# Column attention and two feed-forward layers in float32: four more outputs of the first token pair by seven products

## The chip, the core and the metric

One core of a Trainium2 chip. The metric is the device time of one execution in microseconds (us). TensorE (PE, with its weight loads PEld) does the matrix products into PSUM; VectorE (DVE) and ScalarE (ACT) read PSUM and SBUF; GpSimd (POOL) and SyncE (SP) issue DMAs here. Each engine runs its own queue in program order and waits for others by semaphores.

## The reference, cut to what matters

```python
qn = q / (norm(q, axis=1) + 1e-6);  kn = k / (norm(k, axis=1) + 1e-6)   # q, k, v: 6016 x 256
a = softmax(kn.T @ qn / tau)                                            # 256 x 256
x = v @ a
h = x @ w_in                                                            # 256 -> 2048
x = (h * sigmoid(1.702 * h)) @ w_out                                    # 2048 -> 256
h = x @ moe2_w_in
out = (max(h, 0) + alpha * min(h, 0)) @ moe2_w_out
```

All is float32.

## The kernel before

**Words.** A float32 operand is split into a high part (a rounded copy, by ScalarE) and a low part (the difference, by VectorE), and a product is three matmuls: high by high, high of the weights by low of the data, low of the weights by high of the data. The weights arrive as raw 64-bit words in 16 pieces of 128x512 for each layer (8 of W1I, the input weights, which are multiplied by the softmax first; 8 of W1O, the output weights, in `WO`), and the `Converter` turns each into such a pair: `scale` on ScalarE, then `shift`, `power`, `rest` on VectorE, then either `less` and `low` on VectorE around a ScalarE `copy` (five VectorE steps), or, for an `added` piece, an accumulating DMA on POOL's queue, and later a ScalarE `copy` and a VectorE `split` (four VectorE steps). W1I's pieces 4 to 7 and W1O's 4 to 7 are added.

**Tokens** are worked in six pairs of two column blocks (five pairs of 2x512, one of 2x448), through layer 1 and then layer 2; within a pair, over eight output groups j = 0 to 7. An output group has four outputs (two rows of 128 by two column blocks). Each output is activated by ScalarE, split (`ghi` by ScalarE L876, `glo` by VectorE L882), and multiplied by `WO` into `ps_o`; these second products (`outs.next()`, L814) of group j are emitted between the first products (L785) of group j + 1.

**Two ways of a group.** `direct` takes eight products, 24 matmuls. `quartet` is a Strassen form with seven products, 21 matmuls. It needs four sums of weights (`combine_wi`: VectorE `whole`, `sums_`, ScalarE `high`, VectorE `low`) and four differences of data, T1 to T4 (`prepare`: VectorE difference, ScalarE high, VectorE low). Its products come in the order A11·B11, S1·T1, A12·B21, S2·T2, S3·T3, A22·T4, S4·B22. In the first pair groups 0 to `STRASSEN` - 1 are direct, since weights and differences are not there yet; `STRASSEN` is 6. In the other pairs all groups are quartets.

**How W1I comes.** `emit_w(j)` (in output 1 of groups 0 to 2) and `emit_pair(j)` (outputs 13 and 21, counted 4j + i) multiply the softmax by a piece into the PSUM tile `pw`; ScalarE copies the high part from there, and VectorE makes the low part right behind (L575 and L579; L726 and L727).

**The planner.** Side work is placed at build time. After each direct output `beside(FIRST)` first emits up to `most` of the ScalarE jobs in `put_off`, then VectorE steps until a budget of 2.1 us is used; a quartet has three such places, with budgets `FREE`. Steps come from `bg` (of each kind, 0 = data, 1 = weight sums, only the oldest can go) or from the converter; the converter goes first when its `due` is not later than the step's. A load must be 3 places old before its `scale` (`LOADING`), and an accumulating DMA 3 places before its `copy` (`LANDING`). A step whose ScalarE job is still in `put_off` has to wait. `finish(steps)` emits at once what is left of the steps, wherever it stands. In the code: `LAST = 4 * STRASSEN`, and T1 to T4 are due three or four places before `LAST` and finished before the first quartet.

Of the kernel before, what the change touches and what calls it, by code (L numbers as in the profile page):

```python
# [15 lines left out]
P = 128  # L16
N = 6016
C = 256
# [12 lines left out]
FREE = ((0.7, 2.8, 1.7), (0.0, 0.8, 0.8))  # L31
FIRST = 2.1
AHEAD = 2
QK_PARTS = [1, 3] + [4] * 9 + [2, 2, 2, 1]
TAIL = 12
LOADING = 3
LANDING = 3
STRASSEN = 6
ON_VECTOR = (4, 5, 6, 8)
# [20 lines left out]
def attention_then_two_ffns(ctx: ExitStack, tc: tile.TileContext, q, k, vT, tau, w1i, w1o, w2i, w2o, alpha, outT):  # L60
# [129 lines left out]
    class Converter:  # L190


        STEPS = (("shift", 0.45), ("power", 0.45), ("rest", 0.63), ("less", 0.63), ("low", 0.63))
        ADDED = (("shift", 0.45), ("power", 0.45), ("rest", 0.63))

# [30 lines left out]
        def time(self, piece):  # L226
            if not piece or self.landed():
                return 0.63
            return self.list(piece)[self.at][1]
# [35 lines left out]
        def step(self):  # L265

            if self.waits():
                if not self.open:
                    self.scale(True)
                scalar_work()  # L270
            if not self.next() or self.landed():
                self.settle()
                return 0.63
            if not self.open:
                self.open = self.ready.pop(0)
                self.held = 1
            steps = self.list(self.open)
            do, t = steps[self.at][0], self.time(self.open)
            getattr(self.open, do)()
            self.at += 1  # L280
            if do == "rest":
                self.held = 0
                self.scale()
                if self.ahead:
                    self.load()
            if self.at == len(steps):
                if self.open.added:
                    self.open.sent()
                    self.flying.append(self.open)
                self.open, self.at = None, 0  # L290
            return t
# [17 lines left out]
        def due(self):  # L309
            return min(x.due for x in self.left())  # L310

# [19 lines left out]
    with tc.manual_schedule():  # L331
# [26 lines left out]
        def outer(j, n=1):  # L358
            def pair():
                return tuple(WO[:, j:j + n, h].rearrange("p q a b -> p q (a b)") if n > 1 else flat(WO[:, j, h]) for h in range(2))  # L360
            return Convert(w1o[:, j * PIECE:(j + n) * PIECE].rearrange("p (a n) -> p a n", a=1), pair, added=j > 3)

# [6 lines left out]
        LAST = 4 * STRASSEN  # L369
        PAIRS = {4: 13, 6: min(21, LAST - 2)}  # L370
        for j, x in ia.items():
# [237 lines left out]

        operands, xin2, combining = {}, [], []  # L610

        class Step:
# [7 lines left out]
            def waits(self):  # L620
                return self.needs in put_off

            def run(self):
                if self.waits():
                    scalar_work()
                self.do()
                if self.then:
                    put_off.append(self.then)

        def prepare(l, p):  # L630
# [20 lines left out]
            def minus(nm, a, b):  # L651
# [4 lines left out]
                ("B11", B11), ("B21", B21), ("T1", None), ("T2", None), ("T3", None), ("T4", None), ("B22", B22))}  # L656
            D = 0.63
            early = [
# [18 lines left out]
            if (l, p) == (0, 0):  # L677
                def last():
                    ops["T4"] = operand()
                    tmp["T4"] = tmp["T2"]  # L680
                    minus("T4", B21, "T2")
                steps = [early[i] for i in (2, 3, 6, 7)] + [late[0], Step(D, None, last, hi["T4"])] + [late[i] for i in (4, 5)]
                for x, due in zip(steps, (4, 4, 4, 4, 3, 3, 3, 3)):
                    x.due = LAST - due
                return steps
            return early, late

        def combine(hi, lo, hi_s, lo_s):

            box = {}  # L690

            def whole():
                t = box["t"] = cv.tile([P, 4, P], F32, tag="c", name="t", bufs=2)
                nc.vector.tensor_tensor(t, f32(hi), f32(lo), ALU.add)

            def sums_():
                t = box["t"]
                s = box["s"] = cv.tile([P, 4, P], F32, tag="c", name="s", bufs=2)
                nc.vector.tensor_tensor(s[:, 0], t[:, A21], t[:, A22], ALU.add)
                nc.vector.tensor_tensor(s[:, 1], s[:, 0], t[:, A11], ALU.subtract)  # L700
                nc.vector.tensor_tensor(s[:, 2], t[:, A11], t[:, A21], ALU.subtract)
                nc.vector.tensor_tensor(s[:, 3], t[:, A12], s[:, 1], ALU.subtract)

            def low():
                nc.vector.tensor_tensor(lo_s(), box["s"], f32(hi_s()), ALU.subtract)

            def high():
                nc.scalar.copy(hi_s(), box["s"])

            steps = [Step(0.63, None, whole, kind=1), Step(0.9, None, sums_, high, 1), Step(0.63, high, low, kind=1)]  # L710
            combining.append(steps)
            return steps

        def combine_wi(j):
            return combine(*(WI[:, j, h, :4] for h in range(2)), *(lambda h=h: WI[:, j, h, S1:] for h in range(2)))

        def emit_pair(j):

            conv.need([ia[j], ia[j + 1]])
            for m in range(2):  # L720
# [5 lines left out]
                nc.scalar.activation(hi, src, AF.Copy, scale=rs[:, m:m + 1])  # L726
                nc.vector.scalar_tensor_tensor(lo, src, rs[:, m:m + 1], f32(hi), ALU.mult, ALU.subtract)  # L727

        def emit_w(j):
# [6 lines left out]
            for m in range(2):  # L736
                if j > 1 or m:
                    keep_hi(j, m, pw, m * C)
                    keep_lo(j, m, pw, m * C)

        bg = []
        spare = [0.0]

# [6 lines left out]
        def beside(time, convert=False, place=None, most=None):  # L750

            conv.place()
            now = scalar_work(most)
            late = now if place == 0 else []
# [18 lines left out]
        def finish(steps):  # L773

            while any(s in bg for s in steps):
                s = next(x for x in bg if x in steps) if Convert.deep else bg[0]
                bg.remove(s)
                if s.waits():
                    put_off.remove(s.needs)
                    s.needs()  # L780
# [103 lines left out]
        def direct(j, outs, mid_way):  # L884
# [3 lines left out]
            for i, (f, c) in enumerate((f, c) for f in range(2) for c in range(2)):  # L888
# [11 lines left out]
                mid_way(i)  # L900
                beside(FIRST, most=2 if (j, i) == (STRASSEN - 1, 3) else 3)
                u.low()
                units.append((f, c, u.pair))
            return Outs(0, 0, j, units)

        def quartet(l, p, j, outs, carry):
# [20 lines left out]
            ends = (l, p, j) == (1, NP - 1, NQ - 1)  # L927
            most = 1 if l else 2 if narrow else None
            u11, u22, u21, u12 = (Unit(l, 2 * j + f, c) for f, c in ((0, c0), (1, c1), (1, c0), (0, c1)))
            fork = (l, p, j) != (1, 0, 0)  # L930
            a, b = bank(), bank()
            product(a, j, A11, ops["B11"], n, True, True)
# [20 lines left out]
            if j != 1:  # L953
                beside(FREE[l][0], place=0, most=most)
            if fork:
# [11 lines left out]
            if before:  # L967
                b12.low()
            outs.next()
            product(a, j, S2, ops["T2"], n, False, True)  # L970
            u2 = copy(a)
# [5 lines left out]
            outs.next()  # L977
            beside(FREE[l][1], most=most)
            finish(late[:4])
            product(a, j, S3, ops["T3"], n, False, True)  # L980
            u3 = copy(a)
# [3 lines left out]
            evacuate()  # L985
            beside(FREE[l][2], most=most)
            finish(late)
            u22.act()
            product(a, j, A22, ops["T4"], n, False, True)
# [14 lines left out]
            return Outs(l, p, j, [(0, c0, u11.pair), (1, c1, u22.pair), (1, c0, u21.pair), (0, c1, u12.pair)])  # L1004

        operands[0, 0] = blocks
        conv.ahead = True
# [27 lines left out]
        small = [flat(G), Convert.pool.tile([P, T], F32, tag="top", name="second", bufs=3)]  # L1035
        sums0, pair1 = [], []
        outs, carry = None, []
# [21 lines left out]
        def combining_of(n):  # L1059
            combined[n] = combine_wi(n)  # L1060
            for x in combined[n]:
                x.due = LAST + 3 * ((n or NQ) - STRASSEN) - 1
            bg.extend(combined[n])

        def mid_way(i):
            at = 4 * j + i
            if j < 3 and i == 1:
                if j == 0:
                    conv.need([ob_[0]])
                emit_w(j + 1)  # L1070
            for n, due in PAIRS.items():
                if at == due:
                    emit_pair(n)
                    for m in (n, n + 1):
                        if m >= STRASSEN:
                            combining_of(m)
            if j == 2 and i == 0:
                nc.sync.dma_start(alpha_sb, alpha)
            if at == LAST - 10:
                sums0.extend(prepare(0, 0))  # L1080
                bg.extend(sums0)
            if at == LAST - 2:
                combining_of(0)
            next_pair()

        for j in range(NQ):
            if j:
                conv.need([ob_[j - 1]])
            if j < STRASSEN:
                outs = direct(j, outs, mid_way)  # L1090
                continue
            finish(combined[j])
            finish(sums0)
            next_pair()
# [152 lines left out]
```

## Time and profile before

| | us |
|---|---|
| median of 3 runs (1032.49 to 1033.44) | 1032.55 |
| the profiled execution | 1033.06 |
| its span, first to last instruction | 1031.3 |
| busy PE / DVE / ACT / POOL in the span | 1025.7 / 750.5 / 758.5 / 38.4 |

A share of busy time is an average over stages; the timelines below show who waits at a place. Matmuls overlap, so their single durations (385 ns) are longer than their spacing.

### The profile page before, as it was taken

What the parts mean: (1) busy time and instruction counts of PE and PEld (TensorE: products, weight loads), DVE (VectorE), ACT (ScalarE), POOL (GpSimd) and SP (SyncE); (2) the same over time, 40 slices, a digit from 0 to 9 for tenths busy, and PEclk for the clock granted to TensorE, in tenths of its full rate; (3) what the DMA queues carried; (4) which work ended last, traced back from release to release, by engine and by line L of the source; (5) the groups of instructions that cost most, each with busy time, mean ns of one, the idle gap of its engine ahead of it and who ended that gap; (6) DMA issues with size and microseconds to landing.
All of it is one profiled execution on the core that took longest, in us unless ns stands there. A gap on an engine that the chain in (4) does not pass through costs nothing.

```text
span 1031.3 us, 12536 instructions
## 1 busy us (share of the span) xinstructions
PE 1025.7 (99%) x4634; PEld 865.4 (84%) x4634; DVE 750.5 (73%) x1226; ACT 758.5 (74%) x1273; POOL 38.4 (4%) x50
## 2 busy tenths in 40 slices
PE   9999999999999999999999999999999999999998
PEld 8888888888888888888998888888888888888997
DVE  4788888877778765445637877787877787877766
ACT  6787787778778766666767777777777777867776
POOL 4401000000000000000100000000000000000000
PEclk9999999999999999999999999999999999999999
DMA  9737222224325312003553001001001000000100
GB/s 356 266 106 178 65 74 70 98 80 168 114 89 179 113 41 77 1 1 132 196 168 113 1 21 62 1 21 62 1 21 62 1 18 25 36 0 1 41 1 36
DMA packets 32445, 79.72 MB, mean 77 GB/s; under 512 B 3200, under 2 KB 7808, under 8 KB 32384
## 3 DMA queue, kind: packets, MB, share of 16 engines
q1 hardware_dynamic: 28928, 65.29, 18.3%
q0 software_dynamic: 3456, 13.63, 4.6%
q8 instruction: 36, 0.59, 0.2%
q14 instruction: 25, 0.20, 0.1%
HBM read 52.96 MB, written 23.86 MB: 74 GB/s over the span
## 4 chain that ended last, share of the span: by engine, by line
PE 99%; DMA 0%; SPq 0%; ACT 0%; issue 0%
PE ps_o L814 50%; PE ps_h L785 44%; PE gram L433 4%; PE pw L567 1%; PE pw L723 1%; DMA qk<-in_k 0%; SPq L453 0%; PE nrm L510 0%; ACT s L831 0%; PE bc L532 0%; PE pt L555 0%
## 5 line engine op out<-in xcount | busy, mean ns | idle before, releaser
L814 PE MATMUL ps_o<-ghi,wo 128*128 128x512 f32 (+1 forms) x1536 | 561.0, 385 | 0.0
L785 PE MATMUL ps_h<-x,wi 128*128 128x512 f32 (+1 forms) x2034 | 548.1, 385 | 0.0
L785 PEld LDWEIGHTS ps_h<-x,wi 128*128 128x128 f32 x2034 | 381.2, 188 | 71.9 <-DVE wi L579 0.4
L814 PEld LDWEIGHTS ps_o<-ghi,wo 128*128 128x128 f32 x1536 | 288.4, 188 | 53.7
L814 PE MATMUL ps_o<-glo,wo 128*128 128x512 f32 (+1 forms) x768 | 296.1, 386 | 0.0
L851 DVE TENSOR_TENSOR g<-ps_h,s 128x512 f32<-128x512 f32 (+1 forms) x177 | 120.1, 679 | 103.9 <-PE ps_h L785 63.5
L880 DVE SCALAR_TENSOR_TENSOR glo<-g,sign_sb,ghi 128x512 fp32r<-128x512 f32 (+1 forms) x192 | 141.5, 737 | 55.4 <-ACT ghi L874 51.0
L923 ACT COPY s<-ps_h 128x512 f32<-128x512 f32 (+1 forms) x177 | 102.2, 577 | 106.4 <-PE ps_h L785 102.2
L882 DVE TENSOR_TENSOR glo<-g,ghi 128x512 fp32r<-128x512 f32 (+1 forms) x192 | 126.4, 677 | 65.9 <-ACT ghi L876 65.1
L814 PEld LDWEIGHTS ps_o<-glo,wo 128*128 128x128 f32 x768 | 144.2, 188 | 27.2 <-DVE glo L880 0.3
L874 ACT ACTIVATE ghi<-g,sign_sb 128x512 fp32r<-128x512 f32 (+1 forms) x192 | 137.2, 714 | 16.3 <-DVE g L870 10.9
L876 ACT CAST ghi<-g 128x512 fp32r<-128x512 f32 (+1 forms) x192 | 113.1, 612 | 3.4
L862 ACT ACTIVATE g<-ps_h 128x512 f32<-128x512 f32 (+1 forms) x108 | 63.3, 586 | 41.6 <-PE ps_h L785 41.1
L866 ACT ACTIVATE g<-g,sign_sb 128x512 f32<-128x512 f32 (+1 forms) x97 | 69.4, 716 | 29.2 <-DVE g L851 28.7
L870 DVE SCALAR_TENSOR_TENSOR g<-g,slope_sb 128x512 f32<-128x512 f32 (+1 forms) x97 | 71.6, 738 | 16.7 <-ACT g L866 16.6
L870 DVE SCALAR_TENSOR_TENSOR g<-ps_h,slope_sb,g 128x512 f32<-128x512 f32 (+1 forms) x95 | 69.7, 734 | 0.0
L934 ACT COPY ps_h<-ps_h 128x512 f32<-128x512 f32 (+1 forms) x89 | 50.2, 564 | 26.4 <-PE ps_h L785 26.1
L866 ACT ACTIVATE g<-ps_h,sign_sb 128x512 f32<-128x512 f32 (+1 forms) x95 | 64.3, 676 | 1.9 <-PE ps_h L785 0.2
L862 ACT ACTIVATE g<-g 128x512 f32<-128x512 f32 (+1 forms) x84 | 52.3, 622 | 13.8 <-DVE g L851 13.3
L433 PE MATMUL gram<-qk 128*128 128x256 f32 x156 | 34.3, 380 | 1.0 <-DMA qk<-in_k 1.0
L433 PEld LDWEIGHTS gram<-qk 128*128 128x128 f32 x156 | 29.4, 190 | 5.2 <-issue 1.4
L649 DVE TENSOR_TENSOR x<-t,x 128x512 fp32r<-128x512 f32 (+1 forms) x48 | 32.0, 674 | 0.0
(123 smaller groups left out, 493.5 us busy)
## 6 DMA issues: line engine op xcount, KB each, us to landing
wi<-w2i POOLq DMA_DIRECT2D x8, 896.0 KB, 4.9
xraw<-in_vT SPq DMA_DIRECT2D x10, 512.0 KB, 5.5
x<-ob SPq DMA_DIRECT2D x20, 256.0 KB, 2.9
xraw<-x SPq DMA_DIRECT2D x10, 512.0 KB, 3.7
out_T<-ob SPq DMA_DIRECT2D x20, 256.0 KB, 2.0
qk<-in_q SPq DMA_DIRECT2D x9, 512.0 KB, 10.3
qk<-in_k SPq DMA_DIRECT2D x9, 512.0 KB, 10.6
raw<-in_w1i SPq DMA_DIRECT2D x8, 512.0 KB, 5.0
```

What stands on the lines that cost most here:

```text
L433: nc.tensor.matmul(gram[m][:, :C], tiles[i][:, 1, r, m * P:(m + 1) * P], tiles[i][:, 0, r, :], start=(t == 0), stop=(t == R - 1))
L785: nc.tensor.matmul(ps[:, :n], WI[:, wq, a, blk], x[:, b, :n], start=(start and i == 0), stop=(stop and i == 2), skip_group_check=True)
L814: nc.tensor.matmul(acc_ps[c][d][:, :n], WO[:, j, a, f, d * P:(d + 1) * P], (hi, lo)[b][:, :n], start=(start and i == 0), stop=(stop and i ...
L851: nc.vector.tensor_tensor(self.src, ps[:, :self.n], s[:, :self.n], ALU.add)
L862: nc.scalar.activation(self.g, self.src, AF.Gelu_apprx_sigmoid)
L866: nc.scalar.activation(self.g, self.src, AF.Copy, scale=sign_sb[:, self.f])
L870: nc.vector.scalar_tensor_tensor(self.g, self.src, slope_sb[:, self.f], self.g, ALU.mult, ALU.max)
L874: nc.scalar.activation(self.hi, self.g, AF.Copy, scale=sign_sb[:, self.f])
L876: nc.scalar.copy(self.hi, self.g)
L880: nc.vector.scalar_tensor_tensor(self.lo, self.g, sign_sb[:, self.f], f32(self.hi), ALU.mult, ALU.subtract)
L882: nc.vector.tensor_tensor(self.lo, self.g, f32(self.hi), ALU.subtract)
L923: nc.scalar.copy(s[:, :n], ps[:, :n])
```

## The change

- `STRASSEN` goes from 6 to 4: groups 4 and 5 of the first pair become quartets. Their weight sums are made in the first pair; before, they were made in the second. W1I's second pair of pieces is multiplied at output 15 in place of 21.
- The low parts of W1I are emitted behind the VectorE steps of their place (`lows`, `settle_w`), not ahead. The budget of such a place grows by 0.5 us (outputs 1, 5 and 9) or 1.0 us (13 and 15).
- For pieces 4 to 7, ScalarE also writes a whole float32 copy of `pw` to SBUF. VectorE takes the low part from this copy and the weight sums from it too, so `whole` goes for these groups.
- W1O's pieces 2 and 3 become `added`.
- ScalarE's `high` of a weight sum is held back one place (`aging`).
- T1 to T4 are prepared at output 7 (14 before), are due at places 15, 16, 17, 17, and are finished one by one inside the first quartet (`operands_of`), not before it. The first pair's quartets 4 to 6 have budgets 0.9, 3.1, 2.1 in place of 0.7, 2.8, 1.7.
- A converter piece not yet in flight counts as due 4 places earlier if added, else 1; a step's price in the plan is 0.62 in place of 0.63.

```diff
+MORE = (0, 1), (1, 1), (2, 1)
 AHEAD = 2
 QK_PARTS = [1, 3] + [4] * 9 + [2, 2, 2, 1]
 TAIL = 12
 LOADING = 3
 LANDING = 3
-STRASSEN = 6
+SETTLING = 1
+STRASSEN = 4
...
-            return min(x.due for x in self.left())
+            return min(x.due - (0 if x in self.flying else 4 if x.added else 1) for x in self.left())
...
-            return Convert(w1o[:, j * PIECE:(j + n) * PIECE].rearrange("p (a n) -> p a n", a=1), pair, added=j > 3)
+            return Convert(w1o[:, j * PIECE:(j + n) * PIECE].rearrange("p (a n) -> p a n", a=1), pair, added=j >= 2)
...
-        PAIRS = {4: 13, 6: min(21, LAST - 2)}
+        PAIRS = {4: 13, 6: 15}
...
-                if self.then:
+                if self.then and self.kind and conv.ahead and Convert.deep:
+                    aging.append((conv.now, self.then))
+                elif self.then:
...
-                for x, due in zip(steps, (4, 4, 4, 4, 3, 3, 3, 3)):
-                    x.due = LAST - due
+                for x, due in zip(steps, (-1, 0, -1, 0, 1, 1, 1, 1)):
+                    x.due = LAST + due
...
-            steps = [Step(0.63, None, whole, kind=1), Step(0.9, None, sums_, high, 1), Step(0.63, high, low, kind=1)]
+            steps = ([] if t is not None else [Step(0.62, None, whole, kind=1)]) + [Step(0.9, None, sums_, high, 1), Step(0.62, high, low, kind=1)]
...
-                nc.vector.scalar_tensor_tensor(lo, src, rs[:, m:m + 1], f32(hi), ALU.mult, ALU.subtract)
+                if j + 1 < STRASSEN:
+                    lows.append(lambda hi=hi, lo=lo, src=src, m=m: nc.vector.scalar_tensor_tensor(
+                        lo, src, rs[:, m:m + 1], f32(hi), ALU.mult, ALU.subtract))
+                    continue
+                if not m:
+                    both = xin[1].tile([P, 2, 4, P], F32, tag=f"x{7 + j // 2}", name="whole")
+                    wholes[j], wholes[j + 1] = both[:, 0], both[:, 1]
+                part = both[:, :, 2 * m:2 * m + 2]
+                nc.scalar.activation(part, src, AF.Copy, scale=rs[:, m:m + 1])
+                lows.append(lambda hi=hi, lo=lo, part=part: nc.vector.tensor_tensor(lo, part, f32(hi), ALU.subtract))
...
-                    keep_lo(j, m, pw, m * C)
+                    lows.append(lambda m=m: keep_lo(j, m, pw, m * C))
+
+        def settle_w():
+
+            for do in lows:
+                do()
+            lows.clear()
+            for n in sums_next:
+                combining_of(n)
+            sums_next.clear()
...
+            while aging and conv.now - aging[0][0] >= SETTLING:
+                put_off.append(aging.pop(0)[1])
...
-                beside(FIRST, most=2 if (j, i) == (STRASSEN - 1, 3) else 3)
+                beside(FIRST + (0.5 if (j, i) in MORE else 1.0 if lows else 0), most=2 if (j, i) == (STRASSEN - 1, 3) else 3)
+                settle_w()
...
+        def operands_of(which):
+
+            finish([x for i, x in enumerate(sums0) if (0, 1, 0, 1, 2, 3, 2, 3)[i] <= which])
...
+            free = (0.9, 3.1, 2.1) if narrow and j < NQ - 1 else FREE[l]
...
+            if narrow:
+                operands_of(0)
             product(a, j, A11, ops["B11"], n, True, True)
...
-                x.due = LAST + 3 * ((n or NQ) - STRASSEN) - 1
+                x.due = LAST + 3 * ((n or NQ) - STRASSEN) - 2
...
+        def pairs(at):
+            for n, due in PAIRS.items():
+                if at == due:
+                    emit_pair(n)
+                    sums_next.extend(m for m in (n, n + 1) if m >= STRASSEN)
+            if at == max(LAST - 1, PAIRS[6]):
+                sums_next.append(0)
...
-            if at == LAST - 10:
+            if at == 7:
...
-            finish(sums0)
```

## Rows read from the trace of the kernel before

**Rows 1.** The page: busy us (share) xinstructions by engine, and the chain by engine.
```profile
PE 1025.7 (99%) x4634; PEld 865.4 (84%) x4634; DVE 750.5 (73%) x1226; ACT 758.5 (74%) x1273; POOL 38.4 (4%) x50
...
PE 99%; DMA 0%; SPq 0%; ACT 0%; issue 0%
```
**Rows 2.** The chain in order of time, 56 to 145 us: start us, us, what.
```profile
59.44 0.68 PE ps_h L785 x3
...
61.48 0.82 PE ps_o L814 x3
...
88.37 2.73 PE pw L723 x12
...
96.54 0.68 PE ps_h L785 x3
...
130.56 1.36 PE ps_h L785 x6
...
140.76 1.36 PE ps_h L785 x6
```
**Rows 3.** Timeline of VectorE: start us, us, engine line operation out<-in [idle before <-releaser].
```profile
56.90 0.69 DVE L882 TENSOR_TENSOR glo<-g,ghi 128x512 fp32r<-128x512 f32 x1
58.43 0.48 DVE L579 SCALAR_TENSOR_TENSOR wi<-pw,rs,wi 128x256 fp32r<-128x256 f32 x1 [0.83 <-ACT wi L575]
58.83 0.68 DVE L158 SCALAR_TENSOR_TENSOR p<-raw,p 128x512 f32<-128x512 uint32 x1
59.43 0.68 DVE L182 TENSOR_TENSOR top<-top,wi_hi 128x512 f32<-128x512 f32 x1
60.22 0.69 DVE L185 TENSOR_TENSOR wi_lo<-top,p 128x512 fp32r<-128x512 f32 x1
60.82 0.69 DVE L882 TENSOR_TENSOR glo<-g,ghi 128x512 fp32r<-128x512 f32 x1
```
**Rows 4.** Timeline of ScalarE at the first outputs and at outputs 13 to 15.
```profile
57.92 0.47 ACT L575 ACTIVATE wi<-pw,rs 128x256 fp32r<-128x256 f32 x1
58.29 0.61 ACT L151 CAST wi_hi<-top 128x512 fp32r<-128x512 f32 x1
...
91.14 0.69 ACT L726 ACTIVATE wi<-pw,rs 128x512 fp32r<-128x512 f32 x1 [0.68 <-PE pw L723]
91.72 0.65 ACT L138 ACTIVATE p<-raw 128x512 f32<-128x512 f32 x1
...
97.06 1.14 ACT L645 CAST x<-t 128x512 fp32r<-128x512 f32 x2
```
**Rows 5.** Timeline of TensorE's weight loads in the same first outputs.
```profile
59.05 0.64 PEld L785 LDWEIGHTS ps_h<-x,wi 128*128 128x128 f32 x3
...
61.56 0.19 PEld L814 LDWEIGHTS ps_o<-glo,wo 128*128 128x128 f32 x1 [0.28 <-DVE glo L882]
```
**Rows 6.** Timeline of VectorE at output 13, at T1, at a combination and in quartet 7.
```profile
92.53 0.68 DVE L158 SCALAR_TENSOR_TENSOR p<-raw,p 128x512 f32<-128x512 uint32 x1
93.13 0.42 DVE L142 TENSOR_SCALAR top<-p 128x512 uint32<-128x512 uint32 x1
93.58 0.43 DVE L155 TENSOR_SCALAR p<-top 128x512 uint32<-128x512 uint32 x1
93.93 0.69 DVE L882 TENSOR_TENSOR glo<-g,ghi 128x512 fp32r<-128x512 f32 x1
...
101.52 1.29 DVE L649 TENSOR_TENSOR x<-t,x 128x512 fp32r<-128x512 f32 x2
...
117.87 0.29 DVE L699 TENSOR_TENSOR s<-t 128x128 f32<-128x128 f32 x1
...
118.81 0.69 DVE L882 TENSOR_TENSOR glo<-g,ghi 128x512 fp32r<-128x512 f32 x1
...
138.98 0.69 DVE L851 TENSOR_TENSOR g<-ps_h,second 128x512 f32<-128x512 f32 x1
```
**Rows 7.** Line L162, the accumulating DMAs: time from issue to landing.
```profile
DMA to landing us min/median/max: 3.3/4.9/6.8
```
**Rows 8.** Stretches: us, busy by engine, granted clock, DMA share, GB/s.
```profile
6.00:7.00 1.00, 0.29 (x2) 0.00 (x0) 0.00 (x0) 0.00 (x0) 0.00 (x0) 1.00 1.07 375
60.00:99.27 39.27, 39.27 (x185) 32.78 (x184) 33.45 (x63) 28.89 (x52) 4.62 (x5) 1.00 0.61 160
```

More of the change, by code (lines that the diff above doesn't have):

```diff
@@ L190, in attention_then_two_ffns @@
     class Converter:
-        STEPS = (("shift", 0.45), ("power", 0.45), ("rest", 0.63), ("less", 0.63), ("low", 0.63))
-        ADDED = (("shift", 0.45), ("power", 0.45), ("rest", 0.63))
+        STEPS = (("shift", 0.45), ("power", 0.45), ("rest", 0.62), ("less", 0.62), ("low", 0.62))
+        ADDED = (("shift", 0.45), ("power", 0.45), ("rest", 0.62))
         def __init__(self):
@@ L227, in time @@
             if not piece or self.landed():
-                return 0.63
+                return 0.62
             return self.list(piece)[self.at][1]
@@ L272, in step @@
                 self.settle()
-                return 0.63
+                return 0.62
             if not self.open:
@@ L608, in attention_then_two_ffns @@
         conv.steps(2)
-        operands, xin2, combining = {}, [], []
+        operands, xin2, combining, aging = {}, [], [], []
         class Step:
@@ L620, in waits @@
             def waits(self):
-                return self.needs in put_off
+                return self.needs in put_off or any(self.needs is x for _, x in aging)
             def run(self):
@@ L656, in prepare @@
                 ("B11", B11), ("B21", B21), ("T1", None), ("T2", None), ("T3", None), ("T4", None), ("B22", B22))}
-            D = 0.63
+            D = 0.62
             early = [
@@ L682, in prepare, with combine @@
                 steps = [early[i] for i in (2, 3, 6, 7)] + [late[0], Step(D, None, last, hi["T4"])] + [late[i] for i in (4, 5)]
-                for x, due in zip(steps, (4, 4, 4, 4, 3, 3, 3, 3)):
-                    x.due = LAST - due
+                for x, due in zip(steps, (-1, 0, -1, 0, 1, 1, 1, 1)):
+                    x.due = LAST + due
                 return steps
             return early, late
-        def combine(hi, lo, hi_s, lo_s):
-            box = {}
+        def combine(hi, lo, hi_s, lo_s, t=None):
+            box = {"t": t}
             def whole():
@@ L714, in combine_wi @@
         def combine_wi(j):
-            return combine(*(WI[:, j, h, :4] for h in range(2)), *(lambda h=h: WI[:, j, h, S1:] for h in range(2)))
+            return combine(*(WI[:, j, h, :4] for h in range(2)), *(lambda h=h: WI[:, j, h, S1:] for h in range(2)), wholes.get(j) if j >= STRASSEN else None)
+        lows, wholes = [], {}
         def emit_pair(j):
@@ L738, in emit_w @@
                     keep_hi(j, m, pw, m * C)
-                    keep_lo(j, m, pw, m * C)
+                    lows.append(lambda m=m: keep_lo(j, m, pw, m * C))
[6 more added lines that the diff above has]
+            sums_next.clear()
         bg = []
+        sums_next = []
         spare = [0.0]
@@ L778, in finish @@
                 if s.waits():
-                    put_off.remove(s.needs)
+                    aged = [x for x in aging if x[1] is s.needs]
+                    if aged:
+                        aging.remove(aged[0])
+                    else:
+                        put_off.remove(s.needs)
                     s.needs()
@@ L953, in quartet @@
             if j != 1:
-                beside(FREE[l][0], place=0, most=most)
+                beside(free[0], place=0, most=most)
             if fork:
@@ L969, in quartet @@
             outs.next()
+            if narrow:
+                operands_of(1)
             product(a, j, S2, ops["T2"], n, False, True)
@@ L977, in quartet @@
             outs.next()
-            beside(FREE[l][1], most=most)
+            beside(free[1], most=most)
             finish(late[:4])
+            if narrow:
+                operands_of(2)
             product(a, j, S3, ops["T3"], n, False, True)
@@ L985, in quartet @@
             evacuate()
-            beside(FREE[l][2], most=most)
+            beside(free[2], most=most)
             finish(late)
+            if narrow:
+                operands_of(3)
             u22.act()
@@ L1004, in quartet @@
             return Outs(l, p, j, [(0, c0, u11.pair), (1, c1, u22.pair), (1, c0, u21.pair), (0, c1, u12.pair)])
+        sums0 = []
         operands[0, 0] = blocks
@@ L1035, in attention_then_two_ffns @@
         small = [flat(G), Convert.pool.tile([P, T], F32, tag="top", name="second", bufs=3)]
-        sums0, pair1 = [], []
+        pair1 = []
         outs, carry = None, []
@@ L1070, in mid_way @@
                 emit_w(j + 1)
[L1071 to L1076, printed above, removed]
+                if j + 1 >= STRASSEN:
+                    sums_next.append(j + 1)
+            pairs(at)
             if j == 2 and i == 0:
                 nc.sync.dma_start(alpha_sb, alpha)
-            if at == LAST - 10:
+            if at == 7:
                 sums0.extend(prepare(0, 0))
                 bg.extend(sums0)
-            if at == LAST - 2:
-                combining_of(0)
             next_pair()
@@ L1091, in attention_then_two_ffns @@
                 continue
+            assert not lows and not sums_next
             finish(combined[j])
-            finish(sums0)
             next_pair()
```

## The prediction

> **What bounds the kernel now.** I read the page first: TensorE is busy for 1025.7 of 1031.3 us, and the chain that ended last is 99% TensorE [rows 1]. Next the chain in order of time, which shows the spacing that overlapped durations hide: three 512-column matmuls take 0.68 us, 0.227 each, piece after piece, and a quartet takes 130.56 to 140.76, 10.20 us, which is 45 such matmuls (21 of the first products, 24 of the second) and nothing else [rows 2]. So there is no idle time to win. In the first pair one piece is longer than 0.68, 0.82 at 61.48 [rows 2], where a weight load waits 0.28 for VectorE's low part of an activation [rows 5]. A matmul that goes is worth 0.227 us, and each new wait of TensorE is paid in full. VectorE has 33.5 of 39.3 us busy between 60 and 99 us, ScalarE 28.9 [rows 8]: with 85% busy, their order decides, so the timelines of the two come last.
>
> **Products.** Groups 4 and 5 lose three matmuls each: 6 x 0.227 = 1.36 us, all on the path [rows 2].
>
> **The first low parts of W1I, later (output 1).** Group 1's third weight load (its low part, rows of m = 1) stands in the three loads at 59.05 to 59.69, so it starts near 59.5 [rows 5]. Its source, L579, ended at 58.91 before, and VectorE had idled 0.83 us for it [rows 3]. Now the steps come first: `rest` right behind `glo`, at 57.5; `less` waits for ScalarE's copy, 58.29 + 0.61 = 58.90 [rows 4]; `low` 0.79 later as at 59.43 to 60.22, the low part 0.60 behind that [rows 3]: 60.3, done 60.8. The extra 0.5 us of budget stays unused, since the next piece's load is two places old and three are asked. TensorE waits 60.85 - 59.5 = 1.3 us. `glo` of output 1 ends where it ended before (60.74 + 0.69, against 60.82 + 0.69), so the 0.14 at 61.48 goes: net +1.2. Bounds: 0 if that load had 1.3 us of slack that I don't see, 1.4 if the copy comes later. The later low parts (outputs 5 and 9) have over 1 us in hand after this shift and cost 0. From here all TensorE times are those of before + 1.2.
>
> **VectorE's and ScalarE's work.** Added in the first pair: two weight sums (0.95 for the four small steps, 117.87 to 118.81 less the pitch, and 0.60 for the low part, a pitch that L649's two steps in 1.29 show [rows 6]), 3.1 us; two more VectorE steps in each of two quartets, 2.4. Gone: `whole` for groups 6 and 7 and one step for each of W1O's pieces 2 and 3, 2.4. ScalarE gets four whole copies at a pitch of 0.58 (91.14 to 91.72 [rows 4]) and three more jobs in each new quartet. As a sum this fits. In the second pair VectorE loses 4.3 us beside a TensorE that never waits there: worth 0. The two new accumulating DMAs go behind the others on POOL's queue; landing took 3.3 to 6.8 us [rows 7] and three places are 8.2, so they cost 0, and a microsecond for each microsecond beyond.
>
> **The order in front of the first quartet is what I expect to cost.** I worked the planner by hand. For the kernel before, this gives the order that the rows show (output 13: `rest`, `shift`, `power`, then `glo` [rows 6]). For the changed kernel:
>
> - Outputs 9 to 12: W1I's pieces 6 and 7 and W1O's 3 and 4 go first, being due at 11, 11, 12 and 15 against T1's 15 and T2's 16. Only T1's difference is placed (output 11).
> - Output 13: piece 7's `split`, `rest` of piece 4, then `shift`, `power`, `rest` of W1O's piece 5: the flying piece 3 is due at 16, equal to T2, and a tie goes to the converter.
> - Output 14: `sums_` of group 4 (due 14), `split`, `shift`.
> - Output 15: group 4's `low`, T2's difference, T1's low part, `sums_` of group 5. T1's low part stands behind T2's difference, since only the oldest data step may go.
>
> Now the times. At output 13 ScalarE does high and whole of both halves, then a `scale`, then the copy of piece 7: 91.14 + 1.2, three pitches of 0.58, 0.62 for the copy, end 94.7 [rows 4]. VectorE, free at 91.4, waits for it with its first step. From 94.7 it works without a gap: output 13's five steps, two low parts and `glo`, 4.5 us; output 14's, 2.5 us (pitches 0.60 and 0.45 [rows 6]): 101.7. At output 15 TensorE multiplies pair 6 from 96.54 + 1.2 for 2.73 us, as the pair at 88.37 took [rows 2], so quartet 4 starts at 100.5. Group 4's `low` needs ScalarE's `high`, which stands behind the pair's four copies: second half ready at 100.47, high, whole, then `high` to 102.3. So:
>
> 1. VectorE: `low` 102.3, T2's difference 102.9, T1's low part 103.5 to 104.2. S1·T1's second matmul would start 7 matmuls, 1.6 us, after 100.5: 102.05. Wait 2.2.
> 2. VectorE goes on with `sums_` (0.95), two low parts of pair 6 (1.2), `glo` (0.6), one `power` (0.45), then T2's low part: 107.3 to 108.0. S2·T2's second matmul would be at 107.0. Wait 1.0; the product ends at 108.4.
> 3. ScalarE: copy of S2·T2 to 109.0, copy of W1O's piece, `high` of group 5 to 110.1. VectorE had T3's and T4's differences by then; group 5's `low` waits to 110.15, then `split`, `sums_` of group 6, and T3's low part, last: 112.3 to 113.0. S3·T3's second matmul would be at 110.0 (1.36 of second products, 0.23). Wait 3.0; it ends at 113.45.
> 4. T4's low part follows the copy of S3·T3 and the sum into u22: 114.7 to 115.4, wanted at 115.05. Wait 0.4.
>
> Together 6.6 us. No row of before shows these waits, so the bounds: 0 if the low parts land before they are wanted; above, 8.3, if each of the three ScalarE links (`high` of group 4, of T2, of group 5) comes behind one more job of 0.57 (L645's two in 1.14 [rows 4]). I take 6.6, since each link has its own row.
>
> **Quartets 5 and 6.** Their larger budgets bring the sum into u22 later: before it stood at 138.98 to 139.67 in quartet 7 [rows 6], wanted at 140.76 [rows 2], 1.1 in hand. Budgets grow by 0.2 + 0.3 ahead of it and 0.4 behind the one before: 0.9. Between 0 and 0.9 each; I take 0.2 in all, as the row is the nearer end.
>
> **Sum.** -1.36 + 1.2 + 6.6 + 0.2 = +6.6. Against the profiled execution (1033.06; span 1031.3, 1.8 around it) 1039.7; against the median of 1032.55 the forecast is 1039.2.
>
> [...] In the second from 6 to 7 us TensorE worked 0.29 us and the granted clock stayed at 1.00 [rows 8]. [...]
>
> **Rivals.**
>
> 1. *The operands come in time* (not slower). One mechanism: T1's and T2's low parts are planned before output 15, because the converter finds no piece ready and gives its place away; it decides from the point at which T1's low part ends before 102.05, and then T3's stands before group 5's `low` too. For it: VectorE's sum of work fits, and the converter did wait for loads before. Against: the plan worked by hand has a piece ready at each place from 12 to 14. Time: 1032.55 - 1.36 + 1.2 = 1032.4, or 1031.2 if output 1's wait is hidden too.
> 2. *Half of it*: T1 and T2 late, T3 in time, since group 5's `high` finds ScalarE free. -1.36 + 1.2 + 3.2 = +3.0: 1035.6. Against it: the copy of S2·T2 is fixed to TensorE, and stands ahead of that `high`.
> [...]
>
> **How the numbers follow.** Forecast 0.62, rival 1 0.23, rival 2 0.09, rival 3 0.06. A measurement of this kernel tells about 0.2%, 2.07 us, from no change: 1030.5 to 1034.6. Rival 1 lies within it almost whole; it leaves 0.02 for faster. Of the forecast 0.03 falls within it, should ScalarE be quicker at two places. So faster 0.02, same 0.24, slower 0.74. The forecast's own range is 1036.5 to 1041.5 (the top is -1.36 + 1.4 + 8.3 + 0.6 on 1032.55); to hold 8 in 10 I reach down into rival 1, to 1032.0, and leave out its lower third and rival 3.
>
> **What would show it.** Right: a wait of about 1.3 us of a weight load on the W1I low part (the old L579) near 60 us, and quartet 4 lasting about 16.8 us, with matmuls waiting for VectorE's low parts of T1, T2 and T3 (the old L649) by 2.2, 1.0 and 3.0; VectorE idle before a `split` near 94 us. Wrong: quartet 4 at 10.2 us, or T1's low part before output 15 in VectorE's timeline; then the plan was read wrongly, and with it 6.6 of the sum.

## The result, and the profile after

The changed kernel takes 1045.09 us (median, 1044.53 to 1045.33) against 1032.74 beside it on the same chip: ratio 1.0119, 95% interval 1.0106 to 1.0131, or +12.35 us. The forecast was 1039.2, +6.6. The direction was right, the size was not: the time lies above the stated range of 1032.0 to 1041.5.

The page after, as [rows 1]: TensorE does six matmuls less and is yet busy 5.6 us longer, and VectorE and ScalarE have entered the chain that ended last.

```profile
PE 1031.3 (99%) x4628; PEld 866.2 (83%) x4628; DVE 748.0 (72%) x1224; ACT 763.4 (73%) x1283; POOL 40.1 (4%) x52
PE 97%; DVE 1%; ACT 1%; DMA 0%; issue 0%; SPq 0%; DVEq 0%
```

Where TensorE stood idle, from the table of waits (us in total, times, longest); the kernel before has none of these lines:

```profile
PE ps_h L816 <- DVE x L653: 3.9, 2, 2.0
PE ps_o L845 <- DVE wo L167: 1.2, 1, 1.2
PE ps_h L816 <- DVE wi L581: 1.0, 1, 1.0
...
PE ps_h L816 <- ACT x L649: 0.9, 1, 0.9
PE ps_h L816 <- DVE wi L742: 0.3, 1, 0.3
```

These waits sum to 7.3 us, fewer than were lost. The chain in order of time shows the rest (start, us, what; as [rows 2]). The first line is output 1, the second the pair of pieces 4 and 5, then quartet 4 with pieces of three matmuls:

```profile
60.27 0.50 PE ps_h L816
...
89.11 2.74 PE pw L729 x12
...
107.26 1.28 PE ps_o L845 x3
108.54 1.28 PE ps_h L816 x3
...
118.96 1.37 PE ps_h L816 x3
...
121.50 1.39 PE ps_h L816 x6
```

Three matmuls that took 0.68 us take 1.28. The stretches say why (us, TensorE busy with its matmuls, granted clock, DMA share, GB/s):

```profile
104.00:106.00 2.00, 0.02 (x1) 0.54 0.05 10
106.00:108.00 2.00, 1.97 (x5) 0.50 0.02 4
108.00:110.00 2.00, 2.00 (x6) 0.50 0.00 0
110.00:112.00 2.00, 2.00 (x8) 0.75 0.00 0
...
116.00:118.00 2.00, 1.62 (x7) 0.95 0.46 179
118.00:120.00 2.00, 2.00 (x6) 0.50 0.00 0
120.00:122.00 2.00, 2.00 (x7) 0.69 0.00 0
```

The granted clock fell to 0.50 twice: once inside a wait (0.54 in 104 to 106, where TensorE was busy for 0.02 us), and once behind waits, some 1.4 us after TensorE had gone back to work at 116.38. TensorE is "busy" at 0.50 all the same: for the whole of 108 to 110, with 6 matmuls, where 122 to 124 has 10 at a clock of 1.00.

The account, in spans (1043.6 - 1031.3 = 12.3). The pair of pieces 4 and 5 starts at 89.11 for 88.37: +0.7. That is 1.26 at output 1 (TensorE's pause of 1.16 and a slow first matmul behind it, 0.33 to the next start for 0.227) and 0.20 at output 9, less the 0.14 that goes at 61.48 and the 0.58 by which the first DMA came earlier in this execution, which is chance (TensorE's wait for it is 0.3 here, 1.0 in the trace of before, 0.9 in e11's). The pair of pieces 6 and 7 takes 0.4 longer and ends at 100.23. Quartet 4 runs from 100.23 to 122.18 (half of the piece at 121.50 belongs to the next): 21.95 us for 10.20, +11.75. Quartet 5 and all after take 10.20 again, and the six products give back 1.36. The end comes another 0.9 later than that; 0.6 of it are two long pieces in the second pair (at e10 below), the rest was not located. Sum: 0.7 + 0.4 + 11.75 - 1.36 + 0.9 = 12.4.

Inside quartet 4, TensorE's timeline gives each pause, from where its last matmul should end (start + 0.227) to the next start (last bracket: the idle time shown and its releaser):

```profile
101.15 0.50 PE L816 MATMUL ps_h<-x,wi 128*128 128x512 f32 x1 [0.30 <-DVE wi L742]
...
101.73 0.39 PE L845 MATMUL ps_o<-glo,wo 128*128 128x512 f32 x1
103.29 0.50 PE L845 MATMUL ps_o<-ghi,wo 128*128 128x512 f32 x1 [1.17 <-DVE wo L167]
103.62 0.40 PE L816 MATMUL ps_h<-x,wi 128*128 128x512 f32 x1
106.03 1.22 PE L816 MATMUL ps_h<-x,wi 128*128 128x512 f32 x2 [2.01 <-DVE x L653]
...
112.77 0.39 PE L845 MATMUL ps_o<-ghi,wo 128*128 128x512 f32 x1
114.03 0.49 PE L816 MATMUL ps_h<-x,wi 128*128 128x512 f32 x1 [0.87 <-ACT x L649]
116.38 0.73 PE L816 MATMUL ps_h<-x,wi 128*128 128x512 f32 x2 [1.85 <-DVE x L653]
```

Pair's low part 0.5, W1O's piece 3 1.3, T1 2.2, T3 1.0 + 2.1: 7.1 us. Of the other 4.6 of the 11.75, some 4.2 are matmuls at half speed (an estimate: from stretches of 0.5 us, TensorE worked for 8.4 us at a clock of 0.50). The rest is mostly slow first matmuls behind a pause: from 103.29 to the next start it is 0.33, not 0.227. A pause costs about 0.16 more than the idle time shown, since shown durations (0.39) overlap and starts are 0.227 apart.

Ahead of it, ScalarE's timeline (as [rows 4]) holds the link that I had missed:

```profile
89.13 0.65 ACT L140 ACTIVATE p<-raw 128x512 f32<-128x512 f32 x1
91.88 0.62 ACT L153 CAST wi_hi<-p 128x512 fp32r<-128x512 f32 x1 [2.10 <-PE pw L729]
...
93.56 0.68 ACT L732 ACTIVATE wi<-pw,rs 128x512 fp32r<-128x512 f32 x1
```

The tiles `wi_hi` and `wi_lo` have one buffer each. Pieces 4 and 5 fill them until the pair's last matmul at 91.85, and the copy of piece 6, now asked for before that, waits 2.1 us at the head of ScalarE's queue. All behind it comes later. VectorE waits for it (as [rows 6]), and works without a gap from 97.07 until T1's low part at 105.29, which I had at 103.5:

```profile
92.53 0.69 DVE L167 TENSOR_TENSOR wi_lo<-p,wi_hi 128x512 fp32r<-128x512 f32 x1 [3.36 <-ACT wi_hi L153]
...
97.07 0.69 DVE L167 TENSOR_TENSOR wi_lo<-p,wi_hi 128x512 fp32r<-128x512 f32 x1 [2.45 <-ACT wi_hi L153]
...
102.55 0.69 DVE L167 TENSOR_TENSOR wo<-p,wo 128x512 fp32r<-128x512 f32 x1
...
105.29 0.69 DVE L653 TENSOR_TENSOR x<-t,x 128x512 fp32r<-128x512 f32 x1
```

### The profile page after: what moved, and what is told of

The parts are those of the page before. It is cut to its first block, busy times and chain, and to the rows that moved or that the text cites. A ratio compares the mean times of both kernels' runs of the same rounds, so it can differ in the third digit from the quotient of the medians.

```text
span 1043.6 us, 12543 instructions
## 1 busy us (share of the span) xinstructions
PE 1031.3 (99%) x4628; PEld 866.2 (83%) x4628; DVE 748.0 (72%) x1224; ACT 763.4 (73%) x1283; POOL 40.1 (4%) x52
## 4 chain that ended last, share of the span: by engine, by line
PE 97%; DVE 1%; ACT 1%; DMA 0%; issue 0%; SPq 0%; DVEq 0%
PE ps_o L845 49%; PE ps_h L816 43%; PE gram L435 4%; PE pw L569 1%; DMA qk<-in_k 0%; PE pw L729 0%; ACT wi_hi L153 0%; ACT g L893 0%; DVE p L160 0%; DVE wi L709 0%; ACT L1074 0%; ACT ghi L907 0%; DVE x L653 0%; SPq L455 0%; DVE wo L167 0%
## 5 line engine op out<-in xcount | busy, mean ns | idle before, releaser
L882 DVE TENSOR_TENSOR g<-ps_h,s 128x512 f32<-128x512 f32 (+1 forms) x177 | 120.1, 678 | 108.3 <-PE ps_h L816 63.0
L893 ACT ACTIVATE g<-ps_h 128x512 f32<-128x512 f32 (+1 forms) x104 | 60.9, 585 | 34.7 <-PE ps_h L816 33.9
L893 ACT ACTIVATE g<-g 128x512 f32<-128x512 f32 (+1 forms) x88 | 54.9, 624 | 16.3 <-DVE g L882 16.0
```

Source lines behind the costliest of these rows:

```text
L882: nc.vector.tensor_tensor(self.src, ps[:, :self.n], s[:, :self.n], ALU.add)
L893: nc.scalar.activation(self.g, self.src, AF.Gelu_apprx_sigmoid)
```

## The experiments

The theory: the loss is one of order, late operands in quartet 4 because ScalarE's and VectorE's queues hold other steps ahead of them, and the clock that falls behind the waits. Rivals: the missing buffer alone; the seven products or the added DMAs by themselves. The kernel before ran beside each at 1032.5 (e1 to e4) or 1032.7 (the rest). "Less" is against 1045.09.

**e1: T1 and T2 due at output 13.** (T3 and T4 due at 17, as they were.)

```
-for x, due in zip(steps, (-1, 0, -1, 0, 1, 1, 1, 1)):
+for x, due in zip(steps, (-3, -3, -3, -3, 1, 1, 1, 1)):
```

> T1's and T2's steps are due at place 13 (15 and 16 in the change), so that their low parts stand at outputs 12 and 13; nothing else differs. The theory of the order (the low parts of T1 to T3 stand too late in VectorE's queue, and TensorE's waits for them let its clock fall): the waits for T1 (2.0 us) and T3 (0.9 and 1.9) go and with them most of the 4.3 us at the lower clock; left are output 1's 1.25, W1O's and W1I's waits of 1.2 and 0.3: 1036 to 1038 us. The theory of the buffer (ScalarE's copy of W1I piece 6 waits 2.1 us until pair 4's product has read the one buffer, and that lag is the whole cause): still above 1042.

1037.85 us (ratio 1.0051, 1.0036 to 1.0066): 7.2 less. No matmul waits for a T any more; 1.1 for W1O's piece 3 and 0.6 for a sum's high part stay, and the clock still falls behind these two (e1's stretches, as above):

```profile
104.00:106.00 2.00, 2.00 (x7) 0.77 0.02 2
106.00:108.00 2.00, 2.00 (x6) 0.50 0.87 245
```

The order makes the largest part of the loss; a date in the planner takes it away.

**e2: W1I's piece 6 split into a free slot of the tokens' tiles**, so that its copy need not wait for the pair.

```
-        def wi_tiles():
+        def wi_tiles(j=0):
+            if j == 6:
+                return [xin[1].tile([P, 2, PIECE], F32R, tag="x8", name="wi_hi"), sm.tile([P, 2, PIECE], F32R, tag="wilo", name="wi_lo")]
...
-                    t = wi_whole[j] = wi_first.pop() if wi_first else wi_tiles()
+                    t = wi_whole[j] = wi_first.pop() if wi_first else wi_tiles(j)
```

> The high part of W1I's pieces 6 and 7 goes into another buffer (a free token operand slot), so that ScalarE's copy of piece 6 no longer waits for pair 4's product. The theory of the buffer: VectorE and ScalarE are on time again, the waits of quartet 4 go, at most 1036 us. The theory of the order: T1's low part and W1O's piece come about 2 us earlier, but T2's and T3's low parts still stand behind other steps, the clock still falls: 1041 to 1043.5.

1041.79 us (1.0091, 1.0074 to 1.0108): 3.3 less. The copy goes at once (ScalarE's timeline of e2):

```profile
89.65 0.60 ACT L153 CAST wi_hi<-p 128x512 fp32r<-128x512 f32 x1
```

Here the pauses for the T's stand nearly as the forecast had them (2.2, 1.0, 3.0, 0.4), counted as above: T1 1.7, T2 0.8, T3 1.0 + 2.1, T4 none (TensorE's timeline of e2):

```profile
103.88 0.73 PE L818 MATMUL ps_h<-x,wi 128*128 128x512 f32 x2 [1.43 <-DVE x L655]
...
107.56 0.73 PE L818 MATMUL ps_h<-x,wi 128*128 128x512 f32 x2 [0.66 <-DVE x L655]
...
110.52 0.49 PE L818 MATMUL ps_h<-x,wi 128*128 128x512 f32 x1 [0.86 <-ACT x L651]
112.86 0.84 PE L818 MATMUL ps_h<-x,wi 128*128 128x512 f32 x2 [1.85 <-DVE x L655]
```

Quartet 4 takes 18.53 us: 10.20, pauses of 6.3 (0.6 of them for a sum) and 2.05 more, nearly all at half speed, after T3's wait: the granted clock is 0.83, 0.50 and 0.81 in the three stretches from 112 to 118 us. So this is the kernel that I had predicted, with a fall of the clock on top. The missing buffer is worth 3.3 and does not explain the rest. Of the 3.4 us by which quartet 4 is shorter than in the changed kernel, 0.8 are pauses and 2.6 the part at half speed: most of what the buffer costs comes through the clock.

**e3: the low parts of W1I's pieces 1 to 3 ahead of VectorE's steps again.**

```
-lows.append(lambda m=m: keep_lo(j, m, pw, m * C))
+keep_lo(j, m, pw, m * C)
```

> The low parts of W1I's pieces 1 to 3 are emitted ahead of the steps again, as before the change; the pairs keep the new order. If output 1's wait is 1.25 us of TensorE by itself: 1043.9 (1043.4 to 1044.4), and no wait of a weight load on that low part near 60 us. If the later waits of quartet 4 are fixed to VectorE's queue and swallow it: 1045.1, unchanged.

1043.27 us (1.0102, 1.0087 to 1.0117): 1.8 less, a little below the expected range. The wait on L581 is gone, and output 9's 0.2 with it, which makes 1.3. The other 0.5 is open. In its trace the clock falls once instead of twice (0.56 and 0.58 in 106 to 110 us, 1.00 from 110 on), with nearly the same waits in quartet 4 (4.2, 1.2, 0.8 for 3.9, 1.2, 0.9; the 0.3 more is T4's). But the profiled execution is the fastest of four: 1042.70 at a mean clock of 0.998, the others 1043.26 to 1043.37 at 0.996 and 0.997.

**e4: 25 extra matmuls in quartet 4 in the places of the waits**, into banks that are overwritten; nothing reads them (the edit, shortened).

```
+            if fill: filling(d, 5, ops)          # ahead of the first second products
+            if fill: filling(d, 9, ops)          # ahead of S1·T1
+            if fill: filling(bank(), 11, ops)    # ahead of S3·T3
```

> In quartet 4, TensorE gets 25 extra matmuls whose results are overwritten or never read: 5 ahead of the first second product, 9 ahead of S1*T1, 11 ahead of S3*T3, 5.7 us of work put where it waited 6.2 us. If the waits let the clock fall: it stays at 1.00, the 4.3 us at the lower clock go, and some 0.5 us is added where the filling is too long: 1040.5 to 1042. If the clock falls for another reason, or if the half-speed stretch was hidden behind VectorE anyway: 1044.5 or more.

1043.13 us (1.0103, 1.0088 to 1.0118): 2.0 less, although 25 matmuls, 5.7 us, were added. The granted clock is 1.00 throughout (e4's stretches):

```profile
104.00:106.00 2.00, 2.00 (x10) 1.00 0.08 10
106.00:108.00 2.00, 2.00 (x10) 1.00 0.02 4
```

With matmuls in their place the clock stays at 1.00 where it was 0.50: in the changed kernel the waits brought it down. But of the 4.6 us only 2.0 come back: the full-speed products now wait for T2, T3 and T4 (0.65, 0.48 and 0.30 printed, 1.4 in sum), two of which, T2's and T4's, the slow ones had covered. The time lies between my two expectations: the gain falls short of the 3.1 that the upper end of 1042 asks, and the pauses for T2 and T4, 1.3 in full, are about what is missing.

**e5 and e6: seven products for the last two outputs alone**, the rest of the change kept; e6 with e3's edit as well.

```
-STRASSEN = 4
+STRASSEN = 6
-PAIRS = {4: 13, 6: 15}
+PAIRS = {4: 13, 6: 21}
```

> The first pair's last two outputs alone by seven products, as before; all the rest of the change stays (low words behind VectorE's steps, ScalarE's whole copies, outer pieces 2 and 3 by accumulating DMA). Theory of the order (all the loss lies in the places where TensorE waits, and in the clock that follows them): only output 1's wait of 1.0 to 1.2 us and 0.2 at output 9 stay, so about 1033.9 us (1033.4 to 1034.3). Rival, that accumulating transfers or ScalarE's copies cost time of their own elsewhere: 1035 us or more.

> As the run before it, and the low words of pieces 1 to 3 ahead of VectorE's steps again. Theory of the order: nothing is left that makes TensorE wait, so the time of the kernel before, 1032.5 us within 0.4. Rival (own cost of the rest of the change): 1033.5 us or more.

1036.91 (1.0039, 1.0025 to 1.0053) and 1037.81 us (1.0052, 1.0040 to 1.0065). Both expectations of my theory fell: the rest of the change is not free. e5's trace shows output 1's wait of 1.0 and, at the start of quartet 6, 0.9 and 0.8. e6, with more of its low parts in front, is the slower; its waits:

```profile
PE ps_h L816 <- DVE wi L734: 1.7, 1, 1.7
...
PE ps_h L816 <- ACT wi L712: 0.9, 1, 0.9
PE ps_h L816 <- DVE wi L709: 0.8, 1, 0.8
```

So it is again the order: pair 4's low parts (L734) stand behind VectorE's steps, and the sums of the first quartet, now quartet 6, are late.

**e7: e1, e2 and e3 together.**

> Seven products for the last four outputs, with three of the runs so far joined: first two combinations T1 and T2 due at output 13, W1I piece 6 split into a free slot of the tokens' tiles, low words of pieces 1 to 3 ahead again. Theory of the order: no wait over 0.5 us is left, the granted clock stays at 1.00, and the six matmuls that fall away begin to show: 1031 to 1033 us. Rival, that the waits move to the next late operand (VectorE has too much to do by then): 1035 us or more, with a wait of over 1 us in quartet 4.

1035.64 us (1.0028, 1.0017 to 1.0040): 9.4 less, the best of the versions with all four outputs, and still slower than before. The theory's 1031 to 1033 fell; the rival has the time right, but no wait of over 1 us is printed. In the profiled execution the clock stays at 1.00; two of the other five, at 1036.1 and 1036.2 us, show a mean of 0.998. Quartet 4 takes 12.81 us, from 99.09 to 111.90, with two waits (TensorE's timeline of e7):

```profile
100.52 0.49 PE L847 MATMUL ps_o<-ghi,wo 128*128 128x512 f32 x1
101.69 1.23 PE L818 MATMUL ps_h<-x,wi 128*128 128x512 f32 x3 [0.67 <-ACT wi L714]
...
107.90 0.72 PE L818 MATMUL ps_h<-x,wi 128*128 128x512 f32 x2 [0.66 <-DVE x L655]
```

Idle times of 1.3 us on paper, 2.6 lost: 0.27 ahead of 100.52 is not marked at all, and the slow restart at 101.69 (three matmuls in 1.06) adds 0.4. With the six matmuls' 1.36 given back and some 0.8 lost later, most of it in the second pair (e10, below), that is 2.0, the difference of the spans (1033.3 and 1031.3). So this execution leaves no other cost of the seven products; by the medians e7 is 2.9 above the kernel before.

**e8: as e7, with T1, T2 due at output 14, T3, T4 at 16, and W1O's piece 3 at 14.**

> As the run before it, but the combinations spread (T1 and T2 due at output 14, T3 and T4 at output 16), and W1O piece 3 due at output 14. Theory of the order: no wait in quartet 4, 1031.0 to 1032.5 us, at or below the kernel before. Rival (VectorE is full in these outputs, and whatever goes first makes another step late): 1033.5 us or more.

1040.55 us (1.0074, 1.0061 to 1.0086): the rival. What goes first makes the next step late, here the split of W1I's piece 7. The pair at output 15 waits for it, and the clock falls behind the wait, to 0.50 from 101.5 us on (0.87 in 100 to 102 us, 0.50 in 102 to 104); e8's table of waits:

```profile
PE pw L731 <- DVE wi_lo L167: 2.7, 1, 2.7
```

**e9 and e10: as e7, pieces 6 and 7 multiplied between quartets 4 and 5**; e10 with 0.63 for 0.62 as the planner's time of a step.

```
-PAIRS = {4: 13, 6: 15}
+PAIRS = {4: 13, 6: 19}
+            if j == STRASSEN + 1:
+                emit_pair(6)
+                sums_next.extend((6, 7))
             outs = quartet(0, 0, j, outs, carry)
```

> As e7_t12x8lows (seven products for the last four outputs, no wait over 0.7 us printed, yet 2.6 us lost in quartet 4, where 45 matmuls took 12.8 us for 10.2), but the product of W1I pieces 6 and 7 stands between quartets 4 and 5 and their conversion is due then, so that neither VectorE nor ScalarE has their steps ahead of quartet 4. Theory of the order (before quartet 4 there is more to do on VectorE and ScalarE than there is room, because all that was due by quartet 6 is now due by quartet 4): the loss in quartet 4 goes, and the 1.36 us of the six matmuls show: 1031.3 to 1033.0 us. Rival, that some other cost of the seven products stays whatever the order: 1034.5 us or more.

> As the run before it, with 0.63 for 0.62 as the planner's time of a VectorE step, as before. Theory: two waits of some 0.3 us on the g-adds of VectorE in the second pair of column blocks (near 223 and 295 us in the trace of after) come from the fuller stretches that 0.62 allows; they go, 0.3 to 0.8 us less than the run before it. Rival (they come from something else): the same within 0.3.

1040.67 (1.0076, 1.0064 to 1.0089) and 1039.63 us (1.0065, 1.0051 to 1.0079). Neither theory's mechanism: now the sum's high part, ScalarE's L714, comes last ahead of quartets 4 and 6, behind T4's copy and piece 0's sums. One long wait each (in e9 2.05 and 1.65, in e10 3.8 in sum); in e9's trace the clock falls behind both, to 0.50 in 102 to 104 and in 128 to 130 us. The mean clock of the profiled execution is 0.997 in e9 and 0.998 in e10. TensorE's timeline of e9 at the first of them:

```profile
99.50 1.23 PE L818 MATMUL ps_h<-x,wi 128*128 128x512 f32 x3 [2.05 <-ACT wi L714]
```

And e9's stretches behind it:

```profile
100.00:102.00 2.00, 2.00 (x6) 0.66 1.08 294
102.00:104.00 2.00, 2.00 (x6) 0.50 0.33 125
104.00:106.00 2.00, 2.00 (x10) 0.99 0.00 0
```

e10 gives 1.0 back, more than the 0.3 to 0.8 expected. Of the two long pieces in the second pair (1.66 and 1.67 for 1.36 us, at 223.65 and 295.36 in the changed kernel, where a weight load waits up to 0.4 for VectorE's addition L882) one is gone in e10 and one stays, which is 0.3. The clock may be the rest: e10's five executions run from 1038.46 us at a mean of 1.000 to 1040.16 at 0.997, e9's are all at 0.997. Whether 0.62 makes the long pieces is not settled.

**e11: as e6, all low parts in front, T's prepared from output 14 and due at 22 and 23.** Left of the change: the accumulating DMAs of W1O's pieces 2 and 3, ScalarE's whole copies, the planner's times and budgets, and `aging`.

> The last two outputs alone by seven products, all low words in front as before, the combinations prepared from output 14 and due at 22 and 23 as e6 had not: what is left of the change is the accumulating transfers of W1O pieces 2 and 3, ScalarE's whole copies of W1I pieces 6 and 7, and the planner's times. Theory of the order: these cost nothing where nothing waits for them, so 1032.7 us within 0.6. Rival (they have a cost of their own): 1034 us or more.

1036.32 us (1.0037, 1.0025 to 1.0050): fell again. No wait from 60 to 120 us (TensorE is busy for all of it), none on a DMA's piece; at quartet 6's start the same two waits as in e5 and e6, and at 133.06 one of 0.55 for VectorE's sum L881 (TensorE's timeline of e11):

```profile
122.98 0.73 PE L815 MATMUL ps_h<-x,wi 128*128 128x512 f32 x2 [0.86 <-ACT wi L712]
124.47 0.50 PE L815 MATMUL ps_h<-x,wi 128*128 128x512 f32 x1 [0.76 <-DVE wi L709]
```

The added DMAs thus cost nothing that shows. What makes the sums late was not separated: the planner's altered dates, or `aging`, which holds back just the high part that TensorE waits for.

**e12: the changed kernel with e9's move alone.**

> The changed kernel with one thing altered: the product of W1I pieces 6 and 7 between quartets 4 and 5, as in e9. Theory of the order: output 1's wait stays (1.2 us), the combinations' waits of 2.0 and 1.9 us shrink since ScalarE and VectorE have fewer steps ahead of them, and the clock mostly stays up: 1034 to 1037 us. Rival, that the due dates alone (output 13 and later) make the waits: 1040 us or more.

1038.57 us (1.0056, 1.0044 to 1.0069): 6.5 less, between the two expectations. Five waits of 0.4 to 1.0 us (two for sums' high parts at 1.0), none for a T, and a clock of 1.00 throughout in the trace. Taking pieces 6 and 7 out of the stretch ahead of quartet 4 frees nearly as much as e1's date (7.2).

## Why the prediction was wrong

- **Products, -1.36.** Right: quartets from 5 on take 10.20 us again, and e7's balance needs it.
- **Output 1, +1.2.** Right in kind and nearly in size: the load waits 1.42 on L581, and TensorE's pause is 1.16 (forecast 1.3). A further 0.2 at output 9, which I had at 0.
- **VectorE's order.** The plan worked by hand came out as emitted. The times in it did not: the end of piece 7's copy, forecast at 94.7, was 97.0, because ScalarE's copy of piece 6 waited 2.10 us for pair 4's matmuls. I had looked at what each queue holds, and not at which tile a copy writes and who still reads it. e2 prices that link: 3.3 us.
- **Four waits, 6.6.** In sum 7.1, differently laid: T1 2.2 (forecast 2.2), T3 3.1 (3.0). That T1 agrees is luck: its low part came 1.8 late (105.29 for 103.5), and TensorE wanted it 1.8 later too, held up by two waits that I had not forecast. But T2 and T4 cost none, since TensorE at half speed wanted them later (in e4, at full speed, it waits for both); in their place W1O's piece 3 with 1.3 and the pair's low part with 0.5. With the missed link taken away (e2) T1, T2, T3 stand at 1.7, 0.8 and 3.1.
- **The step that failed: the sum "-1.36 + 1.2 + 6.6 + 0.2", which put the four waits end to end at full clock.** Of quartet 4, 4.6 us were lost beside the pauses, some 4.2 of them at half speed; e4 got 2.0 back with the clock at 1.00. A fall of the clock, rival 3, got 0.06: I weighed it as an alternative to the forecast, when the forecast's own waits could bring it about (in e2, with about those waits, it fell to 0.50 in 114 to 116 us). Neither such a fall nor its cost was shown by any row of the kernel before; the changed kernel showed 8.4 us of work at 0.50, and three matmuls in 1.28 us for 0.68. The row that I had on it, 0.29 us busy in one microsecond at a clock of 1.00 [rows 8], was a single gap: in the changed kernel the granted clock is 0.54 at 104 to 106 us, where TensorE was busy for 0.02 us.
- **The rest.** Rival 1 (operands in time) fell, and so did rival 2 (T3 in time: it cost 3.1). Quartets 5 and 6 (+0.2) showed no wait. On the accumulating DMAs, costed at 0, no wait shows in e11. From the second pair on, "worth 0", some 0.9 was lost instead.
- **What made up the miss of 5.7 us**, by the account in spans: 4.6 lost beside the pauses of quartet 4 (half speed, and slow first matmuls), 0.5 more pauses (7.1 for 6.6), 0.4 in the pair of pieces 6 and 7, 0.9 from the second pair on, less 0.5 up to output 13 (0.7 for 1.2, by the early DMA) and the 0.2 of quartets 5 and 6. By experiment the clock is 2.0 net (e4) and the buffer's link 3.3 (e2). The two overlap, since most of e2's gain is clock, and do not add.

## What to carry to other kernels

When a forecast contains waits of TensorE of about 1 to 2 us close together, price the half-speed stretch behind them in the same sum, with a chance of its own, and then ask which later waits it covers: here, behind 1.17 and 2.01 and behind 0.87 and 1.85, it was 8.4 us of work at a clock of 0.50, some 4.2 us lost, and it covered T2's and T4's waits (0.65 and 0.30 in e4). Before moving a step earlier in an in-order queue, look up which tile it writes and who reads that tile last: here the single buffer of `wi_hi` held ScalarE's copy of piece 6 for 2.10 us, and all behind it, which e2 prices at 3.3 us. And saving matmuls by making their operands elsewhere did not pay here, where the engines that make them had little room before the first use: with VectorE at 85% from 60 to 99 us in the kernel before, every order that was tried moved the late operand to another place, and the best of them (e7) still ended 2.9 us above the kernel before.

## What was not expected of the hardware

- Idle times of TensorE and the clock, by trace: 0.6, 1.0 and 0.4 us ahead of 99.43, 101.62 and 102.77 left it at 1.00 (e12), as did two of 0.7 (e7); behind one of 2.05 (e9), or 1.1 and 0.6, 1.1 us apart (e1), it went to 0.50.
- The fall did not always come while TensorE waited. In the changed kernel it first came inside a wait (0.54 in 104 to 106). In e9 it came after TensorE had gone back to work: back at 99.50, 0.66 in 100 to 102, 0.50 in 102 to 104, 0.99 in 104 to 106, at full work all the while.
- The same waits do not always bring it down: 0.85 and 1.85 for T3 left it at 1.00 in e3, 0.87 and 1.85 brought it to 0.50 in the changed kernel. At quartet 6's start 0.9 and 0.8 came with 0.83 in 120 to 130 us in e5's trace; 0.86 and 0.76 left it at 1.00 in e6's and e11's. Executions of one kernel differ too: e5's profiled one took 1038.15 us at a mean clock of 0.998, its other four 1036.5 to 1037.0 at 1.000. What differs is not settled.
